# Weight rounding in half-size pieces inside the first feed-forward group, in an attention and maxout feed-forward kernel

## The chip, the cores and the metric

One core of a Trainium2 chip. The metric is the device time in microseconds (us) of one execution; lower is better. Engines: TensorE (PE, with its weight loads as PEld), VectorE (DVE), ScalarE (ACT), GpSimd (POOL) and SyncE (SP), which issues all DMAs of this kernel.

## What is computed

The reference is a gated linear attention, whose output is the input of a feed-forward block with three maxed branches:

```python
f = 1.0 / (1.0 + np.exp(-f_logit))
for t in range(S):
    state = f[:, :, t, :, None] * state + np.einsum('bhd,bhe->bhde', k[:, :, t], v[:, :, t])
    y[:, :, t] = np.einsum('bhd,bhde->bhe', q[:, :, t], state)
...
h = np.maximum(np.maximum(x @ w1, x @ w2), x @ w3)
return (h @ w_out).astype(np.float32)
```

q, k, v and f_logit are (4, 8, 768, 48) in float32: 4 batches, 8 heads, 768 steps, head size 48. x has 3072 rows of 384; w1 to w3 are 384 x 768, w_out is 768 x 384. The weights come as 64-bit floats; the kernel makes 32-bit floats of them itself, from the two 32-bit words `lo` and `hi` of each.

## The kernel before, in words

Time is cut into 6 chunks of C = 128 steps. A unit u is one chunk c of one batch b (u = 4 c + b), 24 units in all. Four units (GRP), one chunk of all four batches, make one group of 512 tokens for the feed-forward block; there are 6 groups.

`load` (L105) fetches f, k, q and v of a unit into one of four sets of buffers (NLD), each 192 KB. `gates` (L170) transposes f, k and q on PE (L165), takes the sigmoid on ScalarE (L174), the running product with a floor on VectorE (L178, a scan for each of four pairs of heads), its reciprocal (L181, four as well), and scales k and q on POOL (L189, L191). `pairs` (L195) makes the scores (L202), masks them on VectorE (L206) and transposes the scaled k (L212). `outputs` (L219) multiplies by v (L227), makes the state update (L234, L247 to L250), adds the old state's part (L240), copies the result to yT (L243) and moves it to xT with ten DMAs (L258).

`ffn` (L262) is a generator: 18 steps of six matmuls on 512 tokens (L270; three weight tiles, each run as two records), each followed by a copy (L274) or a maximum (L276), which frees one of two PSUM buffers; then four output steps (L281, L284, L286). While the units of group g+1 are built, the main loop (L308) takes five steps a unit from the generator of group g (`fill`).

`load_weight` (L120) and `round_weight` (L130) bring in the weights: 12 pieces of 768 columns, three raw buffers. Rounding is six VectorE operations (L140 to L149, L154, L156), one on ScalarE (L147) and two on POOL (L150, L151). `weights` (L289) is a generator as well, taken five steps a unit from unit 0 on; whatever is left of it is run out before the first group's `ffn` begins, after unit 3.

The order on each engine comes from the framework's scheduler, which takes instructions by their place in the program, and lets a later one go first where it holds the earlier one for not ready by its own estimates. Each engine then works its list in order. All DMAs are issued from SP's list. If the smallest decay product falls under a limit, a second, general path (L335) computes everything again; it isn't run in these executions.

Of the kernel before, what the change touches and what calls it, by code (L numbers as in the profile page):

```python
# [1 line left out]

# [31 lines left out]
C = 128  # L34
DP = 64
P_MIN = 2.0 ** -64
P_FLOOR = 2.0 ** -80
GATE_PAD = 40.0
# [3 lines left out]
def kernel(  # L42
# [23 lines left out]
    THIRD = DFF // 3  # L66
# [8 lines left out]
    def fast():  # L75
        ctx = ExitStack()
        with ctx:
# [11 lines left out]
            floor = keep.tile([128, C], FP32, name="floor")  # L89
            nc.vector.memset(floor, P_FLOOR)  # L90
            ones = keep.tile([128, 1], FP32, name="ones")
# [13 lines left out]
            def load(u):  # L105
                c, b = divmod(u, B)
                for nm, src in (("f", f_logit), ("k", k), ("q", q), ("v", v)):
# [3 lines left out]

            pieces = [(w_in[i][:, :, n * THIRD:(n + 1) * THIRD],
                       src[:, n * THIRD:(n + 1) * THIRD].rearrange("(kt p) c -> p kt c", p=128))
                      for n in range(3) for i, src in enumerate((moe_w1, moe_w2, moe_w3))]
            pieces += [(w_out[:, 2 * n:2 * n + 2, :],
                        moe_w_out[n * 256:(n + 1) * 256, :].rearrange("(j p) c -> p j c", p=128))
                       for n in range(3)]
            raw = {}

            def load_weight(n):  # L120
                dst, src = pieces[n]
                if src.dtype == FP32:
                    nc.sync.dma_start(out=dst, in_=src)
                else:
                    shape = list(dst.shape)
                    raw[n] = work.tile([128, 2 * 768], U32, name="raw", bufs=3)
                    nc.sync.dma_start(out=raw[n].rearrange("p (a c) -> p a c", a=shape[1]),
                                      in_=src.bitcast(U32))

            def round_weight(n):  # L130
                if n not in raw:
                    return
                dst = pieces[n][0]
                N = 768
                words = raw.pop(n).rearrange("p (n two) -> p n two", two=2)
                lo, hi = words[:, :, 0], words[:, :, 1]


                top = work.tile([128, N], U32, name="top_bits")
                nc.vector.tensor_scalar(top, hi, 3, 0x3FFFFFF8, op0=ALU.logical_shift_left, op1=ALU.bitwise_and)  # L140
                nc.vector.scalar_tensor_tensor(top, hi, 0xC0000000, top, op0=ALU.bitwise_and, op1=ALU.bitwise_or)  # L141
                nc.vector.scalar_tensor_tensor(top, lo, 29, top, op0=ALU.logical_shift_right, op1=ALU.bitwise_or)
# [409 lines left out]
```

## Time and profile before

| what | us |
|---|---|
| three runs | 625.78, 626.01, 629.89; median 626.01 |
| profiled execution | 626.03 |
| its span, first to last instruction | 624.3 |
| PE, DVE, ACT, POOL busy | 526.7, 277.5, 109.0, 121.7 |

The span is the profile's own clock from the first to the last instruction; what lies around it is in the execution's time alone. A line of the profile names the kernel's line, the engine, the operation and `out<-in` by the names of the tiles. "[idle before <-releaser]" is the time in which the engine stood still ahead of the instruction, and what ended it.

### The profile page before, as it was taken

How to read it: one execution, taken by the hardware profiler on the slowest of the kernel's cores; microseconds unless marked ns; L12 is line 12 of the kernel's file. 1: busy time of each engine (PE TensorE's matmuls, PEld its weight loads, DVE VectorE, ACT ScalarE, POOL GpSimd, SP SyncE). 2: the span in 40 equal slices, each digit the busy share in tenths (PEclk: the TensorE clock that was granted, in tenths of full speed). 3: DMA queues.
4: the chain of work that ended last, by engine and by line, in shares of the span. 5: the costliest groups of instructions: out<-in, count | busy, mean ns of one | idle time of the engine just before them, and what ended most of it. 6: DMA issues, size and time to landing. Idle time of an engine off the chain costs nothing.

```text
span 624.3 us, 7153 instructions
## 1 busy us (share of the span) xinstructions
PE 526.7 (84%) x2714; PEld 298.7 (48%) x2714; DVE 277.5 (44%) x453; ACT 109.0 (17%) x189; POOL 121.7 (19%) x104
## 2 busy tenths in 40 slices
PE   6450140279999999999999999999999999999995
PEld 4330130164555655555555556555565555554453
DVE  7569769784255045443234550555423433101110
ACT  3220120121122122121211211221212120110000
POOL 3456456540111011001001110111001011000000
PEclk9999975569999999999999999999999999999999
DMA  9847649024223133313412222333111000010001
GB/s 146 245 127 156 108 126 139 1 43 79 47 49 64 51 63 65 57 34 58 93 28 57 58 52 63 64 52 63 26 27 50 14 14 10 13 55 1 0 13 44
DMA packets 120811, 38.31 MB, mean 61 GB/s; under 512 B 104256, under 2 KB 116544, under 8 KB 120768
## 3 DMA queue, kind: packets, MB, share of 16 engines
q1 hardware_dynamic: 120768, 37.77, 30.0%
q8 instruction: 23, 0.38, 0.3%
q14 instruction: 20, 0.16, 0.1%
HBM read 28.31 MB, written 4.72 MB: 53 GB/s over the span
## 4 chain that ended last, share of the span: by engine, by line
PE 78%; DVE 11%; POOL 6%; SPq 2%; DMA 1%; issue 0%; ACT 0%; POOLq 0%; ACTq 0%
PE p L270 45%; PE p L281 15%; PE tr L165 4%; POOL rest_val L150 4%; PE y L227 4%; PE a L202 3%; PE y L240 3%; POOL rest_val L151 2%; SPq L108 2%; DVE prod L178 2%; DVE inv L181 2%; PE tr L212 2%; DVE w_in L156 1%; DVE rest_bits L145 1%; DVE top_bits L141 1%; PE tr L234 1%
## 5 line engine op out<-in xcount | busy, mean ns | idle before, releaser
L270 PE MATMUL p<-xT,w_in 128*128 128x512 f32 x648 | 292.4, 596 | 0.1
L270 PEld LDWEIGHTS p<-xT,w_in 128*128 128x128 f32 x648 | 117.3, 190 | 125.0 <-issue 123.6
L281 PE MATMUL p<-w_out,hm 128*128 128x384 f32 x288 | 94.4, 488 | 0.0
L181 DVE RECIPROCAL inv<-prod 128x128 f32<-128x128 f32 x96 | 80.9, 902 | 0.0
L178 DVE TENSOR_TENSOR_SCAN prod<-gate,floor 128x128 f32<-128x128 f32 x96 | 40.1, 478 | 89.9 <-ACT gate L174 89.9
L276 DVE TENSOR_TENSOR top<-p,top 128x512 f32<-128x512 f32 x36 | 24.6, 683 | 115.1 <-PE p L270 115.1
L281 PEld LDWEIGHTS p<-w_out,hm 128*128 128x128 f32 x288 | 54.3, 190 | 38.0 <-issue 1.4
L192 POOL COPY ends<-prod 128x4 f32<-128x4 f32 x24 | 6.0, 249 | 288.0 <-DVE prod L178 288.0
L227 PE MATMUL y<-at,v_ld 128*64 128x128 f32 x384 | 32.8, 305 | 24.8 <-DVE at L206 24.8
L212 PE MATMUL tr<-ident,kh 128*128 128x128 f32 x80 | 14.9, 316 | 44.1 <-POOL kh L189 43.3
L276 DVE TENSOR_TENSOR hm<-p,top 128x512 f32<-128x512 f32 x36 | 24.6, 684 | 57.3 <-PE p L270 56.8
L227 PEld LDWEIGHTS y<-at,v_ld 128*64 128x64 f32 x384 | 24.6, 150 | 43.0 <-DVE at L206 26.6
L274 ACT COPY top<-p 128x512 f32<-128x512 f32 x36 | 21.1, 586 | 128.1 <-PE p L270 128.1
L189 POOL TENSOR_TENSOR kh<-kt,inv 128x512 f32<-128x512 f32 x24 | 30.8, 1282 | 54.5 <-DVE inv L181 39.6
L150 POOL TENSOR_TENSOR rest_val<-rest_val,power 128x768 f32<-128x768 f32 x12 | 31.3, 2612 | 40.9 <-DVE power L149 29.1
L206 DVE TENSOR_TENSOR at<-a,mask 128x512 f32<-128x512 f32 x48 | 30.7, 682 | 13.2 <-PE a L202 13.2
L202 PEld LDWEIGHTS a<-qh,kh 48*128 48x128 f32 x384 | 26.5, 210 | 16.0 <-issue 16.0
L191 POOL TENSOR_TENSOR qh<-qt,prod 128x512 f32<-128x512 f32 x24 | 30.4, 1267 | 11.8 <-ACT qt L187 7.3
L212 PEld LDWEIGHTS tr<-ident,kh 128*128 128x128 f32 x80 | 9.6, 156 | 47.4 <-POOL kh L189 44.1
L202 PE MATMUL a<-qh,kh 48*128 48x128 f32 x384 | 31.4, 309 | 0.0
L243 ACT COPY yT<-y 128x512 f32<-128x512 f32 x24 | 14.1, 586 | 95.8 <-PE y L240 84.6
L165 PE MATMUL tr<-ident,f_ld 128*128 128x128 f32 x96 | 17.5, 313 | 12.0 <-DVE st L250 6.5
(47 smaller groups left out, 327.9 us busy)
## 6 DMA issues: line engine op xcount, KB each, us to landing
raw<-in_moe_w_dram SPq DMA_DIRECT2D x9, 768.0 KB, 4.8
f_ld<-in_f_logit_dram SPq DMA_DIRECT2D x24, 192.0 KB, 3.6
k_ld<-in_k_dram SPq DMA_DIRECT2D x24, 192.0 KB, 4.2
q_ld<-in_q_dram SPq DMA_DIRECT2D x24, 192.0 KB, 4.4
v_ld<-in_v_dram SPq DMA_DIRECT2D x24, 192.0 KB, 2.9
out_dram<-o SPq DMA_DIRECT2D x24, 192.0 KB, 1.9
xT<-yT SPq DMA_DIRECT2D x144, 24.0 KB, 1.8
raw<-in_moe_w_out_dram SPq DMA_DIRECT2D x3, 768.0 KB, 4.5
```

What stands on the lines that cost most here:

```text
L150: nc.gpsimd.tensor_tensor(val, val, power.bitcast(FP32), op=ALU.mult)
L165: nc.tensor.transpose(t[:, hp, :], flat[:, hp * 128:(hp + 1) * 128], ident)
L178: nc.vector.tensor_tensor_scan(prod[:, hp, :], gate[:, hp, :], floor, 1.0, op0=ALU.mult, op1=ALU.max)
L181: nc.vector.reciprocal(inv[:, hp, :], prod[:, hp, :])
L189: nc.gpsimd.tensor_tensor(kh, kt, inv, op=ALU.mult)
L202: nc.tensor.matmul(a[:, par, hp, :], lhsT=kh[r, hp, :], rhs=qh[r, hp, :], start=True, stop=True)
L206: nc.vector.tensor_tensor(at[:, par], a[:, par], mask.unsqueeze(1).to_broadcast([C, HP, C]), op=ALU.mult)
L212: nc.tensor.transpose(tr_s[:, hp, :], kh[:, hp, :], ident)
L227: nc.tensor.matmul(y[par * DP:(par + 1) * DP, hp, :], lhsT=v_ld[:, 2 * hp + par, :], rhs=at[:, par, hp, :], start=(hp == 0), stop=(c == 0 ...
L270: nc.tensor.matmul(p, lhsT=w_in[i][:, kt, j * 128:(j + 1) * 128], rhs=xT[:, kt, :], start=(kt == 0), stop=(kt == NK - 1))
L276: nc.vector.tensor_tensor(hm[:, j, :] if i == 2 else top, p, top, op=ALU.max)
L281: nc.tensor.matmul(p[:, 0:DM], lhsT=hm[:, j, i * C:(i + 1) * C], rhs=w_out[:, j, :], start=(j == 0), stop=(j == NJ - 1))
```

## The change

1. Pieces are half as large: one 128-column tile of w1, w2 or w3, or one 128-row tile of w_out, 384 columns a partition. There are 24, with six raw buffers. The order is by column tile j, then by branch, so that it is the order of the steps of `ffn`.
2. Rounding takes one shift-and-mask and one and-or on VectorE, a scaled copy of the low word to integers on ScalarE, an integer add on VectorE, a Square of the high word on ScalarE and a compare-and-multiply on VectorE. POOL has no part in it. Each rounding issues the raw load of the piece six places later.
3. Pieces 0 to 2 are rounded in units 0 to 2. The other 21 are taken one after each step of `ffn` of group 0, two a step in its last six.
4. Scan and reciprocal are one instruction each per unit: gate and floor have a column more per pair of heads (0 and 1.0), where the scan starts again.
5. Loads of units 0 to 3 stand first, then six raw pieces; the load of unit u + 4 is issued after the outputs of unit u. In the first group `gates` of units 2, 3 and 4 stand after the outputs of units 0, 1 and 3, those of unit 1 before the loop.

```diff
-            floor = keep.tile([128, C], FP32, name="floor")
+            floor = keep.tile([128, HP, C + 1], FP32, name="floor")
             nc.vector.memset(floor, P_FLOOR)
+            nc.vector.memset(floor[:, :, 0], 1.0)
+            gate_tiles = [keep.tile([128, HP, C + 1], FP32, name=f"gate{i}") for i in range(2)]
+            for t in gate_tiles:
+                nc.gpsimd.memset(t[:, :, 0], 0.0)
...
+            pieces = [(w_in[i][:, :, j * 128:(j + 1) * 128],
+                       src[:, j * 128:(j + 1) * 128].rearrange("(kt p) c -> p kt c", p=128))
+                      for j in range(NJ) for i, src in enumerate((moe_w1, moe_w2, moe_w3))]
+            pieces += [(w_out[:, j:j + 1, :], moe_w_out[j * 128:(j + 1) * 128, :].rearrange("(j p) c -> p j c", p=128))
+                       for j in range(NJ)]
+            N = DM
+            RAW = 6
             raw = {}
...
+                    raw[n] = work.tile([128, 2 * N], U32, name="raw", bufs=RAW)
+                    nc.sync.dma_start(out=raw[n].rearrange("p (a c) -> p a c", a=dst.shape[1]),
                                       in_=src.bitcast(U32))
...
             def round_weight(n):
...
+                if n in raw:
+                    dst = pieces[n][0]
+                    words = raw.pop(n).rearrange("p (n two) -> p n two", two=2)
+                    lo, hi = words[:, :, 0], words[:, :, 1]
+                    top = work.tile([128, N], U32, name="top_bits")
+                    nc.vector.tensor_scalar(top, hi, 3, 0x3FFFFFF8, op0=ALU.logical_shift_left, op1=ALU.bitwise_and)
+                    nc.vector.scalar_tensor_tensor(top, hi, 0xC0000000, top, op0=ALU.bitwise_and, op1=ALU.bitwise_or)
+                    rest = work.tile([128, N], U32, name="rest_bits")
+                    nc.scalar.activation(rest, lo, AF.Copy, scale=2.0 ** -29)
+                    nc.vector.tensor_tensor(top, top, rest, op=ALU.add)
+                    size = work.tile([128, N], FP32, name="size")
+                    nc.scalar.activation(size, hi.bitcast(FP32), AF.Square)
+                    a = dst.shape[1]
+                    nc.vector.scalar_tensor_tensor(dst, size.rearrange("p (a c) -> p a c", a=a), HI_MIN ** 2,
+                                                   top.bitcast(FP32).rearrange("p (a c) -> p a c", a=a),
+                                                   op0=ALU.is_ge, op1=ALU.mult)
+                load_weight(n + RAW)
...
             def gates(u):
                 f_ld, k_ld, q_ld = (pads[nm][u % NLD] for nm in "fkq")
                 tr_f = transposed(f_ld)
-                gate = work.tile([128, HP, C], FP32, name="gate")
-                nc.scalar.activation(gate, tr_f, AF.Sigmoid)
-                prod = work.tile([128, HP, C], FP32, name="prod", bufs=3)
+                gate = gate_tiles[u % 2]
+                nc.scalar.activation(gate[:, :, 1:], tr_f, AF.Sigmoid)
+                scan = work.tile([128, HP, C + 1], FP32, name="prod", bufs=3)
+                nc.vector.tensor_tensor_scan(scan.rearrange("p a t -> p (a t)"), gate.rearrange("p a t -> p (a t)"),
+                                             floor.rearrange("p a t -> p (a t)"), 1.0, op0=ALU.mult, op1=ALU.max)
+                prod = scan[:, :, 1:]
                 inv = work.tile([128, HP, C], FP32, name="inv")
-                for hp in range(HP):
-                    nc.vector.tensor_tensor_scan(prod[:, hp, :], gate[:, hp, :], floor, 1.0,
-                                                 op0=ALU.mult, op1=ALU.max)
-                for hp in range(HP):
-                    nc.vector.reciprocal(inv[:, hp, :], prod[:, hp, :])
+                nc.vector.reciprocal(inv, prod)
...
             def ffn(g, xT):
                 hm = work.tile([128, NJ, TOK], FP32, name="hm")
+                todo = iter(range(3, len(pieces)) if g == 0 else ())
...
                         else:
                             nc.vector.tensor_tensor(hm[:, j, :] if i == 2 else top, p, top, op=ALU.max)
+                        for n in islice(todo, 2 if j >= NJ - 2 else 1):
+                            round_weight(n)
                         yield
...
-            def weights():
-                for n in range(len(pieces) + 2):
-                    if n < len(pieces):
-                        load_weight(n)
-                    if n >= 2:
-                        round_weight(n - 2)
-                        yield
-
-            AHEAD = 2
-            load(0)
-            load(1)
-            pending = weights()
+            for u in range(4):
+                load(u)
+            for n in range(RAW):
+                load_weight(n)
+            pending = iter(())
             def fill(n):
                 for _ in range(n):
                     next(pending, None)
+            xT = None
             gates(0)
-            xT = None
+            gates(1)
             for u in range(NU):
-                if u + AHEAD < NU:
-                    load(u + AHEAD)
+                first = u < GRP
                 if u % GRP == 0:
                     xT = work.tile([128, NK, TOK], FP32, name="xT")
-                if u + 1 < NU:
+                if u and not first and u + 1 < NU:
                     gates(u + 1)
                 fill(2)
                 pairs(u)
                 fill(1)
                 outputs(u, xT)
+                if u + NLD < NU:
+                    load(u + NLD)
+                if first:
+                    if u < GRP - 2:
+                        gates(u + 2)
+                    elif u == GRP - 1:
+                        gates(u + 1)
+                    if u < 3:
+                        round_weight(u)
                 fill(2)
                 if u % GRP == GRP - 1:
```

## Rows read from the trace of the kernel before

**Rows 1.** Table by stretch, columns: stretch, length, then busy us by engine, clock, DMA.

```profile
20.00:60.00 40.00, 11.64 (x70) 8.17 (x69) 31.15 (x41) 8.11 (x12) 22.45 (x11) 1.00 0.60 160
100.00:140.58 40.58, 15.76 (x122) 11.84 (x122) 34.09 (x51) 6.32 (x11) 21.58 (x15) 0.55 0.27 37
206.56:291.09 84.53, 84.53 (x477) 48.27 (x477) 34.62 (x60) 16.60 (x30) 10.90 (x12) 1.00 0.29 57
```

The engines in each line are PE, PEld, DVE, ACT and POOL; then follow the granted clock as a share of 2.4 GHz, the DMA share and GB/s.

**Rows 2.** Chain that ended last: shares by engine, and its last pieces (start, us).

```profile
PE 78%; DVE 11%; POOL 6%; SPq 2%; DMA 1%; issue 0%; ACT 0%; POOLq 0%; ACTq 0%
...
555.69 46.35 PE p L270 x108
602.04 15.49 PE p L281 x48
```

**Rows 3.** Groups by shape: busy us, mean ns | idle before.

```profile
L181 DVE RECIPROCAL inv<-prod 128x128 f32<-128x128 f32 x96 | 80.9, 902 | 0.0
...
L178 DVE TENSOR_TENSOR_SCAN prod<-gate,floor 128x128 f32<-128x128 f32 x96 | 40.1, 478 | 89.9 <-ACT gate L174 89.9
...
L150 POOL TENSOR_TENSOR rest_val<-rest_val,power 128x768 f32<-128x768 f32 x12 | 31.3, 2612 | 40.9 <-DVE power L149 29.1 <-ACT qt L187 5.9 <-DVE expo L154 5.8
...
L174 ACT ACT_TABLE_LOAD x1 | 1.3, 1283 | 0.8 <-PEq L536 0.8
```

**Rows 4.** Timeline of VectorE, 10 to 35 us: start, us, line.

```profile
13.06 3.35 DVE L181 RECIPROCAL inv<-prod 128x128 f32<-128x128 f32 x4
19.37 0.56 DVE L140 TENSOR_SCALAR top_bits<-raw 128x768 uint32<-128x768 uint32 x1 [2.95 <-DMA raw<-in_moe_w_dram]
19.84 0.55 DVE L145 TENSOR_SCALAR rest_bits<-raw 128x768 uint32<-128x768 uint32 x1
20.31 0.95 DVE L141 SCALAR_TENSOR_TENSOR top_bits<-raw,top_bits 128x768 uint32<-128x768 uint32 x1
21.18 0.55 DVE L154 TENSOR_SCALAR expo<-raw 128x768 uint32<-128x768 uint32 x1
...
31.13 1.28 DVE L206 TENSOR_TENSOR at<-a,mask 128x512 f32<-128x512 f32 x2
```

**Rows 5.** Timeline of all engines near 48 us.

```profile
47.81 1.98 POOL L150 TENSOR_TENSOR rest_val<-rest_val,power 128x768 f32<-128x768 f32 x1 [2.94 <-DVE power L149]
48.06 2.16 DVE L145 TENSOR_SCALAR rest_bits<-raw 128x768 uint32<-128x768 uint32 x1
```

**Rows 6.** Timeline of PE at the end of the head, 112 to 141 us.

```profile
112.05 1.11 PE L212 MATMUL tr<-ident,kh 128*128 128x128 f32 x4 [21.67 <-POOL kh L189]
...
113.89 1.10 PE L234 MATMUL tr<-v_ld,ks 128*64 128x48 f32 x16 [0.73 <-ACT ks L214]
...
123.88 2.57 PE L227 MATMUL y<-at,v_ld 128*64 128x128 f32 x16 [8.89 <-DVE at L206]
126.38 2.08 PE L202 MATMUL a<-qh,kh 48*128 48x128 f32 x16
128.39 1.11 PE L165 MATMUL tr<-ident,f_ld 128*128 128x128 f32 x4
...
136.61 1.16 PE L202 MATMUL a<-qh,kh 48*128 48x128 f32 x16
...
140.58 1.98 PE L270 MATMUL p<-xT,w_in 128*128 128x512 f32 x4
```

**Rows 7.** Timeline of ScalarE: the yT copies of units 2 and 3.

```profile
126.53 0.59 ACT L243 COPY yT<-y 128x512 f32<-128x512 f32 x1 [3.36 <-PE y L227]
136.76 0.59 ACT L243 COPY yT<-y 128x512 f32<-128x512 f32 x1 [1.26 <-PE y L227]
```

**Rows 8.** Timeline: DMA issues of SP, merged where they follow one another.

```profile
12.08 1.14 SPq L108 DMA_DIRECT2D v_ld<-in_v_dram  x1
13.27 2.21 SPq L127 DMA_DIRECT2D raw<-in_moe_w_dram  x3
...
137.37 6.21 SPq L258 DMA_DIRECT2D xT<-yT  x10
```

More of the change, by code (lines that the diff above doesn't have):

```diff
@@ L1 @@
 from contextlib import ExitStack
+from itertools import islice
 import concourse.bass as bass
@@ L37 @@
 P_FLOOR = 2.0 ** -80
+HI_MIN = 1.125 * 2.0 ** -15 * (1 - 2.0 ** -22)
 GATE_PAD = 40.0
@@ L65 @@
     TOK = GRP * C
-    THIRD = DFF // 3
     const = ctx.enter_context(tc.tile_pool(name="const", bufs=1))
@@ L109, in load @@
                                       in_=src[b, :, c * C:(c + 1) * C, :].rearrange("h t d -> t h d"))
[L112 to L117, printed above, removed]
+            pieces = [(w_in[i][:, :, j * 128:(j + 1) * 128],
[5 more added lines that the diff above has]
+            RAW = 6
             raw = {}
             def load_weight(n):
+                if n >= len(pieces):
+                    return
                 dst, src = pieces[n]
@@ L124, in load_weight @@
                 else:
-                    shape = list(dst.shape)
-                    raw[n] = work.tile([128, 2 * 768], U32, name="raw", bufs=3)
-                    nc.sync.dma_start(out=raw[n].rearrange("p (a c) -> p a c", a=shape[1]),
+                    raw[n] = work.tile([128, 2 * N], U32, name="raw", bufs=RAW)
+                    nc.sync.dma_start(out=raw[n].rearrange("p (a c) -> p a c", a=dst.shape[1]),
                                       in_=src.bitcast(U32))
             def round_weight(n):
-                if n not in raw:
-                    return
@@ L133, in round_weight @@
[L133 to L142, printed above, removed]
@@ L144, in round_weight @@
-                rest = work.tile([128, N], U32, name="rest_bits", bufs=1)
-                nc.vector.tensor_scalar(rest, lo, 0x1FFFFFFF, None, op0=ALU.bitwise_and)
-                val = work.tile([128, N], FP32, name="rest_val", bufs=1)
-                nc.scalar.activation(val, rest, AF.Copy, scale=2.0 ** -52)
-                power = work.tile([128, N], U32, name="power", bufs=1)
-                nc.vector.tensor_scalar(power, top, 0xFF800000, None, op0=ALU.bitwise_and)
-                nc.gpsimd.tensor_tensor(val, val, power.bitcast(FP32), op=ALU.mult)
@@ L151, in round_weight @@
-                nc.gpsimd.tensor_tensor(val, val, top.bitcast(FP32), op=ALU.add)
-                expo = work.tile([128, N], U32, name="expo", bufs=1)
-                nc.vector.tensor_scalar(expo, hi, 20, 0x7FF, op0=ALU.logical_shift_right, op1=ALU.bitwise_and)
-                a = dst.shape[1]
-                nc.vector.scalar_tensor_tensor(dst, expo.rearrange("p (a c) -> p a c", a=a), 897.0,
-                                               val.rearrange("p (a c) -> p a c", a=a),
-                                               op0=ALU.is_ge, op1=ALU.mult)
+                if n in raw:
[14 more added lines that the diff above has]
+                                                   op0=ALU.is_ge, op1=ALU.mult)
```

## The prediction

> **What bounds the kernel now.** I read the table by stretch first: busy time of each engine in a few parts of the span [rows 1]. From 140.58 us on TensorE never rests: the second feed-forward group, with four chunks of attention woven in, is 84.53 us long and PE is busy for all of it, VectorE for 34.62. Before 140.58 PE works little (11.64 of 40 us, 15.76 of 40.58) while VectorE works 31.15 and 34.09 us. So the kernel is a head of 140.6 us that no PE work fills, and 483.7 us (624.30 - 140.58) that PE fills. The chain that ended last says the same: PE has 78% of the span, VectorE 11% and POOL 6%, and its last stretch is the sixth group alone, 108 and 48 matmuls without a gap, 46.35 + 15.49 us [rows 2]. Work taken from VectorE after 140.58 is therefore worth nothing; every microsecond by which the first group's matmuls start earlier is worth one.
>
> What makes the head long: no group may start before all twelve weight pieces are rounded and units 0 to 3 are done. In one piece POOL alone multiplies for 2.61 us [rows 3] and adds after that, between VectorE's steps. The masks for unit 0 come on VectorE at 31.13, behind two pieces, though the reciprocals of unit 1 end at 16.41 (13.06 + 3.35) and VectorE then waits 2.95 us for the first raw weights [rows 4]. VectorE and POOL also block one another: while POOL multiplies from 47.81 to 49.79, VectorE's bit mask takes 2.16 us [rows 5] instead of 0.55 [rows 4].
>
> **The change, part by part.** *Which rounding stands ahead of the first group.* Before: 12 pieces of 768 columns. After: 3 pieces of 384, and the other 21 half pieces are spread over the 18 steps of group 0, each three or more steps ahead of its use. The head is then set by attention.
>
> *The head, worked out.* Loads and transposes of units 0 and 1 stay where they are, so I keep 16.41 for the end of unit 1's reciprocals. Both masks take 1.28 us [rows 4], the output matmuls of unit 0 take 2.57 [rows 6] and start after the first mask: 16.4 + 0.6 + 0.7 + 2.6 = 20.3 for the copy of yT of unit 0. Then three more units. What is a unit's pitch? At the end of the old head, where rounding has just run out, the yT copies of two units stand 10.2 us apart (126.53, 136.76) [rows 7]. PE's own work for one unit at the pace of the old head is three sets of transposes 3.3, scores 2.08, kh transposes 1.11, state update 1.10, outputs 2.57 [rows 6]: 10.2 too. VectorE needs about 1.3 + 3.4 + 1.3 + 0.4 = 6.4 a unit and 1.7 to 2.0 for one half piece, so it fits underneath. PE's pace is the lower one: 16 score matmuls take 2.08 us at 126.38 and 1.16 at 136.61, and granted clock is 0.55 on average over 100 to 140.58 [rows 1, 6]; that is the 1.2 GHz level against 2.4. Bounds for the pitch are thus some 7.5 us (PE at the upper level, VectorE nearly the bound) and 13 (waits between the engines that don't overlap). I take 11, nearest to the measured 10.2. yT of unit 3 is at 20.3 + 33 = 53.3, and the first feed-forward matmul follows 3.8 us later as it does now (136.76 to 140.58) [rows 6, 7]: 57. Bounds: 47 and 63.
>
> *What stood ready at 140.58 and won't.* Unit 4's scores, kh transposes, state update and unit 5's gate transposes were done before the first group; at full pace 1.2 + 0.7 + 0.7 + 0.7, about 3 us, now fall inside it. Bounds 0 and 5: +3.
>
> *Rounding inside group 0.* A half piece is one shift-and-mask and three two-input operations on VectorE and two activations on ScalarE; POOL has none. On 768 columns the one-input kind starts its successor 0.47 us later and the two-input kind 0.87 [rows 4]; half of the columns gives at least 0.24 and 0.44, and at most the full-size price. Fixed parts let me take 0.27 and 0.47: 0.27 + 3 x 0.47 = 1.7 us, 21 of them 35 us. A group has 34.6 us of VectorE already [rows 1], so 70, and some 5 for POOL's products of kh and qh, which collide as in [rows 5]: 75 of 84.5. It fits on average, not everywhere: a matmul group has only two PSUM buffers, a step lasts 2.57 us on PE (6 x 0.429, from 46.35 / 108 [rows 2]), and scan with reciprocals holds VectorE for about 4.7. Today, with VectorE busy 41%, PE never waits; at 89% it will at times. I take +7, from 0 to 20; at the full-size price (3.1 us a piece, 65 in all) VectorE would need 105 and the group would be 20 longer. The wait that is new is VectorE's integer add for ScalarE's scaled low word: behind it in VectorE's queue stand the maxima that free PSUM for PE. Its cover is that raw pieces are loaded six ahead, so ScalarE may run early.
>
> *One scan and one reciprocal.* 96 scans at 478 ns and 96 reciprocals at 902 [rows 3] become 24 each of four times the length (516 and 512 columns). Per element nothing changes; three dispatches each of under 0.1 us go. At most 0.5 us a unit on VectorE, hidden by PE after the head, perhaps 1 to 2 us over four units in it: I count nothing, bounds -2 and +1. The longer fills of the floor and the gates lie in VectorE's and POOL's wait for the first load.
>
> *The queue of DMA issues.* 16 loads at 1.1 us each come first, then six raw pieces; a full-size raw issue is 0.74 us (2.21 / 3) [rows 8]. The queue is clear by about 23, later than the yT copy of unit 0 at 20.3, so its xT transfers wait 3 us; nobody needs them before 57. Per unit SP then issues ten xT transfers (6.21 us [rows 8]), four loads and a raw piece, under 9 of 11 us. Each new raw load waits in this queue for its buffer, that is for a rounding, with the next unit's xT transfers behind it. Within the head this rounding is earlier on VectorE than the masks that make that xT, so it costs nothing.
>
> *Sum.* 57 + 3 + 7 + 483.7 = 550.7 us of span. The profiled execution took 626.03 for a span of 624.3, so 1.7 lies around it; its time is the median of the runs shown, 626.01. Forecast: **552 us**.
>
> **Rivals.**
> *VectorE becomes the bound of group 0.* For: 89% by my price, over 100% by the upper one; two PSUM buffers. Against: the rounding operations are short and half of the slack is free. Group 0 lasts 105 instead of 84.5 + 7: 552 + 13 = 565, and 571 if the head's pitch is 13 us as well.
> *ScalarE swaps function tables.* The squares are new beside Sigmoid. The trace shows one table load, 1283 ns [rows 3], for all sigmoids and copies. If Square isn't in that table, up to two loads for each of 21 pieces are 54 us of ScalarE in group 0, on top of some 17 there now [rows 1] and 20 for the new activations: 91, over the 84.5, and PSUM is freed late: about +13 to +20, 565 to 572. The Trainium skill (ScalarE: Activation LUTs, "Table sets: the hidden batching unit") says that the cheap functions come with every set and names relu, copy, identity and abs, while a change of set needs a load; Square isn't in that list, and no run here shows it yet.
> *The clock stays down: slower.* If VectorE holds back each step so that PE has gaps as it had from 100 to 140.58, where the granted clock was 0.55 [rows 1], PE does group 0 at the 1.2 GHz level. By the scores (2.08 against 1.16 us) [rows 6] that is 1.8 times, by the two levels twice: 84.5 us become 152 to 169, and with the waits that cause it (20 instead of 7) the time is 552 + 67 + 13 = 632 to 649. For it: the clock was down for just this reason in the old head. Against: it decides only if the gaps return in every one of the 22 steps and last beyond the group's beginning, and VectorE's worst sum above, 105 us, leaves PE busy for most of the group. Low.
> *The head isn't shortened as much.* If the order of VectorE's queue puts the first rounding in front of the masks of unit 0 again, it waits for raw weights that now land behind 16 loads, near 24 us: +7, 559. This belongs to the forecast's upper side.
>
> **How the numbers follow.** Forecast and its near side (535 to 562) 0.65, VectorE bound 0.20, table swaps 0.06, clock down 0.04; 0.05 for a head that is shorter than all I allow (PE at 2.4 GHz from 20 us on, 530). The range: low 535 is a start at 47, 3 for unit 4 and no wait in group 0 (47 + 3 + 483.7 + 1.7); high 578 is the VectorE case with a slow head and the late raw weights (571 + 7). A measurement of this kernel can tell about 1%; faster by more than that needs only 6 of the 84 us saved in the head: 0.94. Same 0.02, slower 0.04.
>
> **What would show it.** Right: the first feed-forward matmul near 57; yT copies of units 0 to 3 about 11 us apart from 20; PE full again from group 1 with 84.5 us a group; POOL without the 2.6 us products; VectorE near 90% in group 0, with PE waits of some 7 us there. Wrong: a first matmul after 70, PE idle over 20 us in group 0, more than one table load, or a granted clock near 0.5 after group 0 has begun.

## The result, and the profile after

The change is faster: 555.34 us (median of four runs, 553.92 to 557.42) against 626.20 beside it, a ratio of 0.8862 with a 95% interval of 0.8824 to 0.8900. Forecast were 552 us, range 535 to 578. The profiled execution took 555.56 us for a span of 553.3; the span fell by 71.0 us.

Table by stretch of the kernel after, columns as in [rows 1]; the first feed-forward matmul starts at 68.70 and group 0 ends at 151.20:

```profile
0.00:20.00 20.00, 12.63 (x82) 9.66 (x82) 15.51 (x28) 6.00 (x9) 7.35 (x17) 0.87 0.97 212
20.00:47.00 27.00, 18.79 (x188) 14.48 (x186) 24.13 (x31) 13.40 (x27) 7.77 (x8) 0.82 0.62 153
47.00:68.70 21.70, 18.82 (x164) 14.21 (x164) 20.99 (x30) 9.01 (x18) 5.85 (x7) 0.72 0.59 139
68.70:97.00 28.30, 28.30 (x66) 12.20 (x65) 13.85 (x29) 7.36 (x15) 0.00 (x0) 0.94 0.69 181
97.00:120.00 23.00, 22.19 (x123) 12.37 (x122) 22.70 (x40) 12.72 (x25) 3.66 (x5) 1.00 0.32 95
120.00:151.20 31.20, 28.96 (x130) 17.11 (x129) 12.39 (x20) 5.13 (x10) 2.25 (x2) 0.89 0.43 98
151.20:235.74 84.54, 84.54 (x478) 48.28 (x477) 34.35 (x36) 16.60 (x30) 10.56 (x12) 1.00 0.26 57
```

The last row is the second group: 84.54 us with PE busy throughout, 84.53 before [rows 1]. From the end of group 0 on, both kernels take 402.1 us (624.3 - 222.24 and 553.3 - 151.20). So the whole gain lies ahead of that point, and the two stretches up to it can be laid side by side, first of the kernel after, then of the kernel before:

```profile
0.00:151.20 151.20, 129.69 (x745) 80.03 (x746) 109.56 (x173) 53.63 (x101) 26.88 (x37) 0.88 0.59 144
```

```profile
0.00:222.24 222.24, 131.33 (x746) 81.26 (x747) 137.92 (x214) 40.75 (x65) 80.78 (x59) 0.88 0.50 98
```

PE does the same work in both (745 and 746 records, 129.69 and 131.33 us). What went is its idle time: 222.24 - 131.33 = 90.9 us before, 151.20 - 129.69 = 21.5 after. That is 69.4 of the 71.0 us. This sum, PE's busy time plus its idle time up to the end of group 0, is the measure by which the runs below are read.

The chain that ended last, shares by engine (before: [rows 2]):

```profile
PE 85%; DVE 8%; issue 3%; ACT 2%; POOL 1%; DVEq 0%; ACTq 0%; POOLq 0%
```

POOL's 6% are 1% now, VectorE's 11% are 8%. Groups by shape, busy us and mean ns (before: [rows 3]):

```profile
L183 DVE RECIPROCAL inv<-prod 128x512 f32<-128x512 f32 x24 | 80.4, 3351 | 1.8
...
L179 DVE TENSOR_TENSOR_SCAN prod<-gate,floor 128x516 f32<-128x516 f32 x24 | 29.5, 1229 | 90.0 <-ACT gate L177 88.0 <-issue 1.9
...
L152 DVE CUSTOM_DVE_ANT_0 top_bits<-top_bits,rest_bits 128x768 uint16<-128x768 uint16 x24 | 13.9, 587 | 0.4
...
L177 ACT ACT_TABLE_LOAD x1 | 1.3, 1283 | 0.8 <-PEq L543 0.8
```

There is one table load, as before, so the squares cost no swap. The four scans of a unit were 4 x 478 = 1912 ns and are 1229, the reciprocals were 4 x 902 = 3608 and are 3351. The integer add appears as an operation on twice as many 16-bit elements, 587 ns.

Timeline of ScalarE, the yT copies of units 0 to 3 (before: [rows 7]):

```profile
20.31 0.59 ACT L245 COPY yT<-y 128x512 f32<-128x512 f32 x1 [2.68 <-PE y L229]
28.96 0.59 ACT L245 COPY yT<-y 128x512 f32<-128x512 f32 x1 [0.35 <-PE y L229]
38.73 0.59 ACT L245 COPY yT<-y 128x512 f32<-128x512 f32 x1 [1.95 <-PE y L229]
46.95 0.56 ACT L245 COPY yT<-y 128x512 f32<-128x512 f32 x1
```

Unit 0 is where it was forecast (20.3), and the pitch is (46.95 - 20.31) / 3 = 8.9 us on average. The queue of DMA issues on SP has another pitch (before: [rows 8]):

```profile
20.93 7.14 SPq L260 DMA_DIRECT2D xT<-yT  x10
...
30.25 0.66 SPq L115 DMA_DIRECT2D v_ld<-in_v_dram  x1
31.01 1.17 SPq L136 DMA_DIRECT2D raw<-in_moe_w_dram  x1
32.27 7.21 SPq L260 DMA_DIRECT2D xT<-yT  x10
...
43.51 6.21 SPq L260 DMA_DIRECT2D xT<-yT  x10
...
54.06 7.36 SPq L260 DMA_DIRECT2D xT<-yT  x10
```

Of the last ten, one alone (timeline of a narrow window):

```profile
57.79 1.73 SPq L260 DMA_DIRECT2D xT<-yT  x1
```

A unit holds this queue for 10.6 to 11.3 us: ten xT transfers, in three of the four units 7.1 to 7.4 us against 6.21 before, and four loads and a raw piece, 4.0 to 4.3 us from the end of one xT to the next. In each of these three units one issue of the ten takes 1.42 to 1.73 us and the nine others 0.5 to 0.62; what makes the one long isn't shown. Unit 3's xT is therefore issued at 54.06, 6.6 us after its copy ended at 47.5. And PE (before: [rows 6]):

```profile
47.57 1.22 PE L204 MATMUL a<-qh,kh 48*128 48x128 f32 x6 [4.83 <-POOL kh L191]
...
68.28 0.49 PE L204 MATMUL a<-qh,kh 48*128 48x128 f32 x4 [1.35 <-POOL kh L191]
68.70 3.31 PE L273 MATMUL p<-xT,w_in 128*128 128x512 f32 x4
...
117.94 0.66 PE L168 MATMUL tr<-ident,q_ld 128*128 128x128 f32 x4 [0.81 <-ACT gate L177]
...
128.95 0.43 PE L229 MATMUL y<-at,v_ld 128*64 128x128 f32 x2 [1.81 <-DVE at L208]
129.82 0.98 PE L229 MATMUL y<-at,v_ld 128*64 128x128 f32 x13 [0.43 <-DVE at L208]
...
131.77 1.95 PE L242 MATMUL y<-qh,st 48*48 48x128 f32 x16
133.65 17.63 PE L286 MATMUL p<-w_out,hm 128*128 128x384 f32 x48
```

The first feed-forward matmul at 68.70 waits for nothing. Ahead of it in PE's list stands attention work of units 4, 5 and 6; from 47.00 to 68.70 PE is busy for 18.82 of 21.70 us. So SP's queue isn't the only thing between yT and this matmul: it starts 14.6 us after SP began with the xT of unit 3 (54.06), where before it was 3.2 us (137.37 to 140.58) [rows 6, 8]. Inside group 0 PE waits three times, 0.81 + 1.81 + 0.43 = 3.05 us, and the last two rows are slow: 1.95 us for what takes 1.08 at full pace, 17.63 for 48 matmuls that took 15.75 in the timeline of the first group of before. Granted clock there, and in a stretch ahead of group 0 (table by stretch):

```profile
50.00:55.00 5.00, 5.00 (x22) 3.41 (x22) 5.00 (x5) 2.17 (x5) 1.09 (x2) 0.50 0.84 166
130.00:135.00 5.00, 5.00 (x48) 4.00 (x47) 2.39 (x6) 0.59 (x1) 0.00 (x0) 0.57 0.22 43
```

The clock was 1.00 from 97 to 120, and 0.57 of 2.4 GHz, near the 1.2 GHz level, in the five microseconds after the waits for VectorE. That costs 0.87 + 1.88 = 2.8 us. Group 0 also begins slowly: its first four records take 3.31 us, where before they took 1.98 [rows 6], another 1.3 us; the granted clock from 68.70 to 72 is 0.58.

### The profile page after: what moved, and what is told of

Read it like the earlier page. It is cut to its first block, busy times and chain, and to the rows that moved or that the text cites. A ratio compares the mean times of both kernels' runs of the same rounds, so it can differ in the third digit from the quotient of the medians.

```text
span 553.3 us, 7062 instructions
## 1 busy us (share of the span) xinstructions
PE 525.2 (95%) x2714; PEld 297.6 (54%) x2714; DVE 248.2 (45%) x322; ACT 121.9 (22%) x225; POOL 66.5 (12%) x82
## 4 chain that ended last, share of the span: by engine, by line
PE 85%; DVE 8%; issue 3%; ACT 2%; POOL 1%; DVEq 0%; ACTq 0%; POOLq 0%
PE p L273 47%; PE p L286 17%; PE tr L168 5%; PE a L204 4%; PE y L229 4%; PE y L242 3%; DVE inv L183 3%; PE tr L236 2%; PE tr L214 2%; DVE prod L179 1%; POOL kh L191 1%; DVE at L208 1%; DVE top_bits L148 1%; DVE top_bits L152 1%; DVE top_bits L147 1%
## 5 line engine op out<-in xcount | busy, mean ns | idle before, releaser
L286 PE MATMUL p<-w_out,hm 128*128 128x384 f32 x288 | 96.3, 495 | 0.0
L183 DVE RECIPROCAL inv<-prod 128x512 f32<-128x512 f32 x24 | 80.4, 3351 | 1.8
L179 DVE TENSOR_TENSOR_SCAN prod<-gate,floor 128x516 f32<-128x516 f32 x24 | 29.5, 1229 | 90.0 <-ACT gate L177 88.0
L204 PEld LDWEIGHTS a<-qh,kh 48*128 48x128 f32 x384 | 25.3, 193 | 25.9 <-issue 16.8
L191 POOL TENSOR_TENSOR kh<-kt,inv 128x512 f32<-128x512 f32 x24 | 32.1, 1336 | 37.8 <-DVE inv L183 36.7
L289 ACT COPY o<-p 128x384 f32<-128x384 f32 x24 | 11.5, 479 | 88.8 <-PE p L286 88.8
L193 POOL TENSOR_TENSOR qh<-qt,prod 128x512 f32<-128x512 f32 x24 | 28.3, 1181 | 21.2 <-ACT qt L189 21.2
L242 PE MATMUL y<-qh,st 48*48 48x128 f32 x320 | 23.0, 283 | 0.0
L216 ACT COPY ks<-tr 128x512 f32<-128x512 f32 x20 | 11.7, 586 | 50.1 <-PE tr L214 50.1
L177 ACT ACTIVATE gate<-tr 128x512 f32<-128x512 f32 x24 | 14.3, 597 | 36.5 <-PE tr L168 36.5
```

The source lines that it names most:

```text
L179: nc.vector.tensor_tensor_scan(scan.rearrange("p a t -> p (a t)"), gate.rearrange("p a t -> p (a t)"), floor.rearrange("p a t -> p (a t)") ...
L183: nc.vector.reciprocal(inv, prod)
L191: nc.gpsimd.tensor_tensor(kh, kt, inv, op=ALU.mult)
L193: nc.gpsimd.tensor_tensor(qh, qt, prod, op=ALU.mult)
L204: nc.tensor.matmul(a[:, par, hp, :], lhsT=kh[r, hp, :], rhs=qh[r, hp, :], start=True, stop=True)
L242: nc.tensor.matmul(y[r, hp, :], lhsT=st[r, hp, :], rhs=qh[r, hp, :], start=False, stop=(hp == HP - 1), skip_group_check=True)
```

## The experiments

All were timed beside the kernel before, which took 626.1 to 626.5 us. In the table, "end" is the end of group 0 in the profiled execution, "busy" and "idle" are PE's up to there. In all of them but the last the span is the end plus 402.0 to 402.4 us.

| run | us | first feed-forward matmul | end | busy | idle |
|---|---|---|---|---|---|
| before | 626.2 | 140.6 | 222.2 | 131.3 | 90.9 |
| after | 555.3 | 68.7 | 151.2 | 129.7 | 21.5 |
| 1 new arithmetic alone | 574.6 | 89.2 | 170.6 | 131.9 | 38.7 |
| 2 new place, old arithmetic | 588.1 | 73.7 | 182.0 | 134.1 | 48.0 |
| 3 one scan alone | 620.1 | 137.5 | 219.5 | 132.6 | 86.9 |
| 4 after, four scans | 555.3 | 64.2 | 149.9 | 125.7 | 24.2 |
| 5 after, 21 pieces not rounded | 550.1 | 71.9 | 145.6 | 127.1 | 18.6 |
| 6 after, loads later | 553.0 | 50.9 | 147.7 | 124.3 | 23.5 |
| 7 after, nine raw buffers | 555.9 | 78.1 | 152.3 | 129.4 | 22.9 |
| 8 after, loads on POOL's queue | 545.7 | 51.4 | 142.1 | 122.5 | 19.6 |
| 9 as 8, xT on two queues | 548.0 | 52.8 | 143.6 | 123.4 | 20.2 |
| 10 after, full-size pieces | 551.6 | 73.1 | 146.0 | 125.3 | 20.7 |
| 11 8 and 10 together | 547.5 | 52.8 | 141.0 | 121.5 | 19.5 |

**1. The new arithmetic alone.** The kernel before, pieces of 768 columns and their place ahead of the first group unchanged:

```diff
-                nc.vector.scalar_tensor_tensor(top, lo, 29, top, op0=ALU.logical_shift_right, op1=ALU.bitwise_or)
...
-                nc.gpsimd.tensor_tensor(val, val, power.bitcast(FP32), op=ALU.mult)
-                nc.gpsimd.tensor_tensor(val, val, top.bitcast(FP32), op=ALU.add)
...
+                rest = work.tile([128, N], U32, name="rest_bits")
+                nc.scalar.activation(rest, lo, AF.Copy, scale=2.0 ** -29)
+                nc.vector.tensor_tensor(top, top, rest, op=ALU.add)
...
```

> The kernel before with the new rounding arithmetic alone, in its old full-size pieces, all twelve ahead of the first group. If most of the gain is that rounding became cheap and left POOL (theory), a piece costs VectorE about 0.5 + 3 x 0.87 = 3.1 us instead of some 9.4 us of elapsed time in the old head (12 pieces in 113 us), so twelve pieces are 37 us beside 31 us of attention: first feed-forward matmul at 80 to 88, time 566 to 574. If most of it is that rounding left the head for group 0 (rival), this run keeps over half of the old head: first matmul after 100, time over 588.

574.57 us, ratio 0.9165 [0.9130, 0.9199]. Table by stretch of this run, head and group 0:

```profile
0.00:89.22 89.22, 50.50 (x322) 37.10 (x322) 76.56 (x129) 37.28 (x53) 17.18 (x26) 1.00 0.85 176
89.22:170.57 81.35, 81.35 (x425) 44.85 (x425) 28.37 (x49) 13.71 (x25) 8.11 (x9) 1.00 0.46 75
```

That is 0.6 us over the range I had named. The arithmetic by itself is worth 626.4 - 574.6 = 51.8 us, nearly all of it in the head; group 0 has no wait. POOL's busy time up to the end of group 0 falls from 80.78 to 17.18 + 8.11 = 25.29 us, and with it the steps in which VectorE and POOL wait for each other. VectorE is busy for 76.56 of the 89.22 us of head that are left.

**2. The new place with the old arithmetic.** The kernel after, with the old operations on 384 columns, POOL's product and sum among them (VectorE has seven operations in the old rounding, not six as stated above):

```diff
-                    nc.vector.tensor_tensor(top, top, rest, op=ALU.add)
...
+                    nc.gpsimd.tensor_tensor(val, val, power.bitcast(FP32), op=ALU.mult)
+                    nc.gpsimd.tensor_tensor(val, val, top.bitcast(FP32), op=ALU.add)
...
```

> The changed kernel with the old arithmetic (seven VectorE and two POOL operations and one activation a piece) on its half-size pieces. Theory: the place alone is not enough, since VectorE was already at 90 to 100% from 97 to 132 us with the cheap arithmetic; with some 2.6 us on VectorE and 2.4 us of POOL that blocks it, 21 pieces are about 100 us beside 35 of attention in a group of 84: group 0 becomes 30 to 50 us longer, time 580 to 605. Rival: TensorE's work hides it, time under 565.

588.07 us, ratio 0.9383 [0.9348, 0.9419]. Its head and its group 0:

```profile
0.00:73.68 73.68, 45.92 (x397) 35.21 (x397) 60.92 (x98) 23.11 (x40) 33.25 (x42) 0.83 0.69 163
73.68:182.04 108.36, 88.16 (x366) 45.51 (x365) 83.67 (x150) 20.44 (x40) 51.86 (x47) 0.90 0.39 96
```

The first matmul is as early as after's, within 5 us, but group 0 is 108.36 us long and PE stands still for 20.2 of them. This is what the rival "VectorE becomes the bound of group 0" looks like when it comes true, though VectorE doesn't hold PE up alone: PE waits 9.7 us for VectorE's maxima and masks, and 10.4 us for ScalarE's gates and its copy of k. ScalarE is busy for only 20.44 us; its list has the rounding's conversion ahead of them, which waits for VectorE (7.31 us at 155.86). So the place alone is worth 38 us, the arithmetic alone 52, both together 71 and not 90: each removes partly the same wait. "Place" stands here for all of the change but its arithmetic; of that, the order of loads and gates was never undone by itself. From either side, what the second edit adds is 19 us (place, run 1 to after) and 33 us (arithmetic, run 2 to after).

**3. One scan and one reciprocal, in the kernel before.**

```diff
-                for hp in range(HP):
-                    nc.vector.tensor_tensor_scan(prod[:, hp, :], gate[:, hp, :], floor, 1.0,
...
+                nc.vector.tensor_tensor_scan(scan.rearrange("p a t -> p (a t)"), gate.rearrange("p a t -> p (a t)"),
+                                             floor.rearrange("p a t -> p (a t)"), 1.0, op0=ALU.mult, op1=ALU.max)
```

> The kernel before with one scan and one reciprocal a unit and nothing else. Theory: hidden by TensorE after the head, at most 1 to 2 us in the head: 623 to 627, no change by the 1% bound. Rival: the four-fold dispatch sits on the chain of each unit of the head and is worth over 6 us: under 620.

620.06 us, ratio 0.9904 [0.9875, 0.9933], a gain of 6.3 us in the medians; its seven executions lie in two groups, 618.8 to 620.1 and 622.7 to 623.4, and the profiled one, 623.31, shows half of the gain. This is more than I expected, and under 2%. Timelines of VectorE and POOL near the gates of one unit, first before, then in this run:

```profile
101.26 4.50 DVE L178 TENSOR_TENSOR_SCAN prod<-gate,floor 128x128 f32<-128x128 f32 x4
...
101.48 1.80 POOL L150 TENSOR_TENSOR rest_val<-rest_val,power 128x768 f32<-128x768 f32 x1 [3.63 <-DVE power L149]
103.37 1.80 POOL L151 TENSOR_TENSOR rest_val<-rest_val,top_bits 128x768 f32<-128x768 f32 x1
```

```profile
96.62 1.22 DVE L180 TENSOR_TENSOR_SCAN prod<-gate,floor 128x516 f32<-128x516 f32 x1
97.76 2.09 DVE L144 TENSOR_SCALAR top_bits<-raw 128x768 uint32<-128x768 uint32 x1
...
96.84 2.60 POOL L154 TENSOR_TENSOR rest_val<-rest_val,power 128x768 f32<-128x768 f32 x1 [3.63 <-DVE power L153]
```

In both, POOL's product starts 0.22 us after the first scan. Before, the four scans then take 4.50 us and the product 1.80; here the one scan is through in 1.22 and it is the product that takes 2.60, and VectorE's next operation, a bit mask of 0.55, 2.09. I read it so that POOL comes in between two instructions of VectorE, of which four scans offer more. The Trainium skill (SBUF — State Buffer, "Who interferes with whom") says that a VectorE instruction with two SBUF inputs contends with a GpSimd instruction that reads SBUF, and that issue order decides who is held up; these rows agree for the scan, by 4.50 against 1.22.

That this makes the head shorter isn't shown. Up to the end of group 0 the scans of nine units take 11.1 us here and 19.5 before, but the rounding's first two operations, a shift and an and-or, take 30.9 instead of 22.2, and VectorE's busy time is 138.68 us against 137.92. The time moved to other instructions; what the gain comes from stays open.

**4. Four scans and four reciprocals, in the kernel after.** The same edit undone.

```diff
-                nc.vector.reciprocal(inv, prod)
...
+                for hp in range(HP):
+                    nc.vector.reciprocal(inv[:, hp, :], prod[:, hp, :])
```

> The changed kernel with four scans and four reciprocals a unit again. Theory: VectorE gets 0.2 to 0.3 us more a unit, in a head and a group 0 where it is nearly the bound: 0 to 3 us over the changed kernel, 555 to 559. Rival: the long instructions block the queue for 3.35 us at a time and the short ones would let masks and maxima in between: up to 3 us under it, 552 to 555.

555.32 us, ratio 0.8869 [0.8822, 0.8916]: no difference from after. With POOL's products out of the rounding the single scan is worth nothing here. First matmul and PE's busy time moved by 4 us each, and the end by 1.3.

**5. What the rounding in group 0 costs.** Pieces 3 to 23 aren't rounded; POOL fills their weights with 0.03, so the result has other weights than the reference's.

```diff
+                    if n >= 3:
+                        nc.gpsimd.memset(dst, 0.03)
+                    else:
...
```

> The changed kernel without the arithmetic of pieces 3 to 23: POOL fills their weight tiles with a constant, so these weights are left out of the computation; loads, queue and order stay. It shows what the rounding inside group 0 still costs. Theory: the two waits of TensorE for the masks near 118 and 129 us (0.8 + 1.8 + 0.4) and the lower clock that follows (130 to 136, some 2.9 us) go: 3 to 8 us less than the changed kernel, 547 to 552. Rival: VectorE's 97 to 132 us at full load held back much more than these waits, also in the head: over 12 us less, under 543.

550.13 us, ratio 0.8773 [0.8739, 0.8808]. Table by stretch, up to the end of group 0:

```profile
0.00:145.64 145.64, 127.09 (x746) 79.67 (x747) 73.69 (x89) 33.28 (x59) 32.45 (x58) 0.92 0.60 149
```

VectorE has 35.9 us less to do there (109.56 - 73.69), which is 1.7 us for each of the 21 pieces, as the prediction priced them; the kernel is 5.2 us shorter. That is close to the 3.05 us of waits and 2.8 us of slower clock read from after's own trace. It is an estimate of what anything done about the rounding can still bring, as POOL's fills are new here and PE's order moved too (first matmul at 71.9).

**6. Loads of units 4 to 7 issued after the outputs of unit 3**, so that SP has only xT and raw pieces in the head:

```diff
-                if u + NLD < NU:
+                if first:
+                    for m in range(NLD) if u == GRP - 1 else ():
+                        load(m + NLD)
+                elif u + NLD < NU:
                     load(u + NLD)
```

> The changed kernel with the loads of units 4 to 7 issued after the outputs of unit 3, so that SP's queue holds only xT transfers and raw weights until then. Theory A, SP's queue sets the start of group 0 (xT of unit 3 was issued at 54.1, 6.5 us after its copy was done): the first feed-forward matmul comes at 50 to 60 instead of 68.7. Theory B on the sum: TensorE's work is conserved, as the attention of units 4 and 5 that stood ahead of group 0 now falls inside it, and only idle time and slow clock of 47 to 68.7 can be won: time 548 to 556. Rival: the twelve us of the earlier start are won whole: 541 to 545.

553.02 us, ratio 0.8801 [0.8760, 0.8842]. The first feed-forward matmul, PE's timeline:

```profile
50.86 2.05 PE L273 MATMUL p<-xT,w_in 128*128 128x512 f32 x2 [7.36 <-DMA xT<-yT]
```

It comes 17.8 us earlier, and the median is 2.3 us lower, with intervals that overlap. The attention work that stood ahead of it stands behind it now; PE's idle time is 23.5 us against 21.5, and 5.4 us of its busy time went. So an early first matmul isn't the gain in itself. The order did move when SP's queue became shorter, and the matmul now waits for xT. That the scheduler put the attention work first because it expected xT late is argued from this; its estimates aren't in the trace. PE's pace is in it: in after PE works at 0.50 of the clock from 50 to 55 us on this attention work, and four transposes take 1.11 us there; woven into group 0 they take 0.60 to 0.65 here.

**7. Nine raw buffers for six**, so that raw loads run further ahead:

```diff
-            RAW = 6
+            RAW = 9
```

> The changed kernel with nine raw buffers instead of six. Theory: VectorE idles at 70 to 76 and 87 to 92 us because the next raw pieces come late, and is then full from 97 to 132; with three more pieces at hand some of this work moves forward, the waits of TensorE near 118 and 129 shrink: 1 to 5 us less, 550 to 555. Rival: the three more loads ahead of the first xT transfers delay SP's queue by 2 us and everything behind it: 555 to 559.

555.94 us, ratio 0.8859 [0.8825, 0.8893]: no gain, against my theory. Its group 0:

```profile
78.08:152.33 74.25, 74.25 (x317) 39.27 (x317) 43.41 (x76) 22.12 (x43) 5.73 (x6) 1.00 0.41 108
```

PE has no wait left in group 0 and the clock stays at 1.00, as the theory had it. But the yT of unit 3 came at 51.93 instead of 46.95, and the head gave back what group 0 gained. Two things differ in this head: three more raw issues stand in SP's queue ahead of the first xT (its xT of unit 3 begins 1.8 us later, at 55.88), and eleven pieces instead of eight are rounded before group 0. Which of them holds yT back wasn't tried.

**8. The later loads on POOL's queue.** SP keeps the first loads, the xT transfers and the outputs:

```diff
-                    nc.sync.dma_start(out=pads[nm][u % NLD][:, :, 0:D],
+                    (nc.sync if u < NLD else nc.gpsimd).dma_start(out=pads[nm][u % NLD][:, :, 0:D],
...
-                    nc.sync.dma_start(out=raw[n].rearrange("p (a c) -> p a c", a=dst.shape[1]),
+                    (nc.sync if n < RAW else nc.gpsimd).dma_start(out=raw[n].rearrange("p (a c) -> p a c", a=dst.shape[1]),
```

> The changed kernel with the loads of units 4 to 23 and the raw pieces from 6 on issued by POOL's queue, so that SP has only xT and output transfers after the first 22. Theory A: xT of unit 3 is issued when its copy is done, near 47, first feed-forward matmul before 60. Theory B: the sum falls by what TensorE idles today before group 0, 2 to 8 us: 547 to 553. Rival: POOL's issues cost more than SP's and hold up kh and qh on POOL and so the attention: over 556.

545.73 us, ratio 0.8699 [0.8659, 0.8739]: 9.6 us under after, more than expected, and the fastest of all. The first matmul, and the table by stretch up to the end of group 0:

```profile
51.38 2.04 PE L273 MATMUL p<-xT,w_in 128*128 128x512 f32 x2 [1.45 <-DMA xT<-yT]
```

```profile
0.00:142.11 142.11, 122.51 (x746) 74.32 (x747) 110.17 (x173) 53.20 (x101) 69.62 (x90) 0.95 0.56 153
```

The wait for xT, 7.36 us in run 6, is 1.45. PE's idle time fell by only 1.9 us, to 19.6; its busy time fell by 7.2, from 129.69 to 122.51, for the same records (745 and 746), at a mean clock of 0.95 for 0.88. Most of this gain is PE's pace, not waits: the transposes that take 1.11 us near 50 in after take 0.60 to 0.66 at 41 to 45 here. The price is on POOL, busy for 69.62 us instead of 26.88, its issues counted; a load's issue there takes 887 to 924 ns, and POOL has the room. The run changes more than the list that issues: the transfers of POOL's queue went as 6,944 packets and all others of the kernel as 35,552, where after has 124,416. Whether part of the gain comes from that wasn't tried; run 6, which leaves the packets as they were, has the early first matmul but not the whole gain.

**9. As 8, with the xT of the odd heads issued by ScalarE in the first four units.**

```diff
-                        nc.sync.dma_start(out=xT[row % 128:row % 128 + n, row // 128, b * C:(b + 1) * C],
+                        (nc.scalar if u < GRP and h % 2 else nc.sync).dma_start(
...
```

> The kernel of the later loads and raw pieces on POOL's queue, and in the first four units half of the xT transfers issued by ScalarE's queue, the other half by SP's. In the run without the second half SP issued the 21 transfers of units 2 and 3 without a pause from 39.2 to 53.4 and the first feed-forward matmul came at 51.4. Theory: SP's queue still bounds the start; with half of it the first matmul comes at 46 to 49, and the time falls by 1 to 4 us, 541 to 545. Rival: what bounds it now is VectorE and POOL for unit 4, and ScalarE's issues (0.6 us each) delay its copies: 545 to 550.

548.04 us, ratio 0.8752 [0.8713, 0.8790]: not better, and inside the rival's range. The two queues for units 2 and 3, and ScalarE, in timelines of narrow windows:

```profile
43.84 3.04 SPq L260 DMA_DIRECT2D xT<-yT  x5
50.25 3.04 SPq L260 DMA_DIRECT2D xT<-yT  x5
```

```profile
43.85 4.38 ACTq L260 DMA_DIRECT2D xT<-yT  x5
48.27 0.60 ACT L177 ACTIVATE gate<-tr 128x512 f32<-128x512 f32 x1 [4.46 <-PE tr L168]
...
49.66 0.57 ACT L245 COPY yT<-y 128x512 f32<-128x512 f32 x1
```

The two queues do issue beside each other: SP takes 0.61 us a transfer, alone it took 0.62 [rows 8], ScalarE 0.88, and the ten transfers of unit 2 are out in 4.4 us instead of 6.2. But SP then stands still from 46.9 to 50.25, because the yT of unit 3 comes at 49.66; in run 8 it came at 44.74. ScalarE's own work waits behind its issues, as the rival had it: the gate for 4.46 us, and the copy of yT starts 2.0 us after PE's outputs of unit 3 end (46.29 + 1.36 = 47.65). The rest of the delay is in PE, which began these outputs at 46.29 instead of 42.67; what that hangs on stays open.

**10. Full-size pieces in the new place.** 768 columns, three raw buffers, three pieces ahead, one piece after every second step:

```diff
...
-            N = DM
-            RAW = 6
+            N = 2 * DM
+            RAW = 3
...
-                        for n in islice(todo, 2 if j >= NJ - 2 else 1):
+                        for n in islice(todo, 1 if (3 * j + i) % 2 == 0 else 0):
```

> The changed kernel with pieces of the old size (768 columns), three of them rounded ahead and nine inside group 0, one at every second step; arithmetic, order and queue as changed. Theory: the size alone is worth little, since VectorE spends 3.1 us on one full piece and 3.4 on two halves, but three full pieces ahead of the group are 4 us more of VectorE in the head, and group 0 has 8 us less: 551 to 558, within 1% of the changed kernel. Rival: the half size is what lets maxima and masks in between and gets the first weights in time: over 561.

551.56 us, ratio 0.8807 [0.8771, 0.8842], 3.8 us under after, with intervals that just overlap. The half size isn't needed. From 100 to 135 us:

```profile
100.00:135.00 35.00, 35.00 (x200) 19.69 (x200) 26.09 (x29) 11.79 (x19) 7.07 (x6) 1.00 0.41 93
```

PE never waits there, where after has its waits. Not size alone differs: three whole pieces are placed ahead of group 0, twice the columns of after, and the other nine are spread evenly over its 18 steps. Which of the two brings the 3.8 us wasn't tried.

**11. Runs 8 and 10 together.**

> Pieces of the old size inside group 0, and the later loads and raw pieces on POOL's queue. Theory: the two gains come from different places (4 us from fewer and longer VectorE instructions in group 0, 10 us from SP's queue) and add up in part: 541 to 545, no slower than 545.7 of the half pieces on POOL's queue. Rival: both are won from the same idle time of TensorE between 47 and 70 us: 545 to 549.

547.50 us, ratio 0.8737 [0.8708, 0.8765]: the gains don't add, and the time lies in the rival's range. Group 0 ends 1.1 us earlier than in run 8 (140.97), with the same idle time; what is left, 404.6 us instead of 402.1, is longer behind the last output matmuls (span end minus 520.61 + 15.64: 9.4 us, in run 8 6.9), which nothing here explains.

## Why the prediction was right, and which of its steps weren't

The time came out 3 us above the forecast, well inside the near range, and the mechanism is the forecast one: the rounding leaves the head, PE's idle time there goes, everything after group 0 stays as it is. But two of the sum's terms were off by about 10 us each, and cancelled. Part of that isn't luck, since attention work that moved ahead of group 0 makes the start later and the group shorter. That the two sizes come so near each other is luck.

- **First yT at 20.3, masks of unit 0 ahead of the rounding:** measured 20.31. The rival of a late first rounding fell with it. The end is right by luck: the masks came at 14.63 on VectorE, not 16.4, while the output matmuls, with transposes between them, lasted from 16.93 to 20.28, not 2.6 us.
- **Pitch 11 us, yT of unit 3 at 53.3:** pitch 8.9, yT at 46.95. I had taken the pace of the end of the old head, where the granted clock was 0.55; from 20 to 47 us it was 0.82 now. PE was busy for 18.79 of these 27.00 us and VectorE for 24.13, so the pitch is nearer to VectorE's work than to PE's, as my lower bound of 7.5 had it.
- **First matmul 3.8 us after it, at 57:** this step failed; it came at 68.70. The sentence that failed stands under the queue of DMA issues: "under 9 of 11 us", which "costs nothing". A unit took SP 10.6 to 11.3 us, because ten xT issues take up to 7.4 us, and the loads with the raw piece, for which "under 9" leaves 2.8, take 4.0 to 4.3. Against a pitch of 8.9 that makes SP's queue the slowest part of the head, and the xT of unit 3 was late by 6.6 us. The matmul came 21.8 us after yT instead of 3.8; beyond SP's 6.6 us the other 11.4 are the attention work that stood ahead of it in PE's list, a term the sum didn't have. Runs 6 and 8, which take loads out of this queue, move that work too and bring the first matmul to 51.
- **"+3" for what stood ready at 140.58:** the wrong sign. More attention work stood ahead of group 0, not less: 432 matmul records, where before it were 322. Without its waits and its two slow stretches group 0 took 82.5 - 3.05 - 2.8 - 1.3 = 75.3 us, 6 less than before (222.24 - 140.58 = 81.7).
- **"+7" of PE waits in group 0:** 3.05 us of waits and 2.8 of slower clock, 5.9 together; run 5 puts it at 5.2. The right size, and with the slow start of 1.3 us nearer still. VectorE's share was overrated, 89% forecast and 48.9 of 82.5 us measured, since 8 pieces, not 3, had been rounded by 68.70, in VectorE's gaps in the head, and since its own attention work is less in group 0 (28.37 us before) than the 34.6 that I took from the second group. In the densest stretch, 97 to 120, it was 22.70 of 23.
- **One scan, counted as nothing:** nothing in the new kernel (run 4). In the old head it is worth up to 6 us (run 3), outside my bounds of -2 and +1; beside POOL four short scans are dearer than one, but why the kernel gets faster stays open.
- **483.7 us unchanged after the start:** from the end of group 0 on unchanged to 0.1 us.
- In sum, for the profiled execution: start +11.7, group 0 82.5 instead of 91.7 (3 + 7 + 81.7), thus -9.2, and 0.6 more around the span: +3.1.

The rivals: VectorE didn't bound group 0, but the old arithmetic stretches it to 108 us (run 2), so the price per piece was what decided. No table swaps: one load, 1283 ns. The Trainium skill (ScalarE: Activation LUTs, "Table sets: the hidden batching unit") names functions that come with every set, without Square; the trace shows that here it needs no load beside Sigmoid and Copy. The clock did fall for some microseconds after PE's waits, as that rival had it, but not for a group. The sign I named for "wrong", a first matmul after 70, nearly came (68.70), and it was a bad sign: run 6 shows that its place is worth little as long as PE has other work to do first.

## What to carry to other kernels

When a head is short of work for the bounding engine, price its busy time and its idle time up to a point behind which nothing changes; the place of one instruction, such as the first matmul, moves by 18 us without the end moving by more than 4. Price a queue of DMA issues per round, with every transfer in it and some long issues among them, and set it against the pitch of the round that you expect, not against a slower one. Making work cheap and moving it under cover overlap: the new place took 38 us off with the old arithmetic and 19 more after the new. The cover only holds work that is cheap enough: group 0 took 108 us with the old arithmetic and 82.5 with the new.

## What the runs showed of the hardware that was not expected

- Ten xT issues on SP took 6.21 us before, and 7.1 to 7.4 us in three of four units after, one issue of the ten 1.42 to 1.73. Issued from two queues at once, five took 3.04 us on SP beside 4.38 on ScalarE (run 9).
- Four scans of 128 columns beside POOL's products took 4.50 us, one of 516 columns 1.22; VectorE's busy time in the whole run didn't fall with it (run 3).
- The 32-bit integer add runs as an operation on 768 elements of 16 bits for 384 columns, 587 ns; on 768 columns (run 10) it is 1536 elements and 1100 ns, so its price follows the columns.
- The same 745 or 746 matmul records up to the end of group 0 took PE 121.5 to 132.6 us, depending on the kernel (run 2's stretch holds 760). Of the 9 us between after and the fastest run, 7 are this.
- The granted clock of a stretch isn't PE's pace by itself. From 20 to 60 us it reads 1.00 in the kernel before [rows 1], but four transposes take there what they take at 128.39 [rows 6], where it is near 0.5, and not the 0.60 of full pace:

```profile
39.58 1.11 PE L165 MATMUL tr<-ident,f_ld 128*128 128x128 f32 x4 [3.14 <-DVE st L250]
```
